# Fused attention and MLP on one core: key and query transposes by DMA from batch 3 on, and unread matmuls in the gaps of the head

## The chip, the cores and the metric

The kernel runs on one core of a Trainium2 chip. A core has five engines with a queue of instructions each, worked off strictly in order: TensorE (PE in the profile: matrix multiplications, and transposes as a multiplication with an identity matrix), VectorE (DVE), ScalarE (ACT), GpSimd (POOL) and SyncE (SP, which here only issues transfers). Sixteen DMA engines move data; transfers are issued from a queue of SyncE, ScalarE or GpSimd. SBUF is the on-chip memory of 128 partitions; PSUM is the small memory into which TensorE writes its results.

The metric is the device time of one execution in microseconds; less is better. Times of one kernel agree within some 0.3%.

## What is computed

Attention with a few extra "beacon" keys and values in front, then a two-layer MLP with an ELU between the layers. The reference, cut to what matters:

```python
B, H, S, Nb, D = 8, 8, 576, 16, 64
k_all = concatenate([beacon_k, k], axis=2)           # 592 keys per head
v_all = concatenate([beacon_v, v], axis=2)
scores = matmul(q, k_all.T) / sqrt(D)                # causal in the 576, beacons always seen
a = exp(scores - scores.max(-1)); a /= a.sum(-1) + 1e-9
x = matmul(a, v_all).transpose(0, 2, 1, 3).reshape(B * S, H * D)   # 4608 x 512
h = x @ w_in                                         # 512 x 2048
g = where(h > 0, h, exp(min(h, 0)) - 1)
out = g @ w_out                                      # 2048 x 512
```

All inputs and the output are float32 in memory. The kernel computes in bf16 and fp16.

## The kernel before

The unit of attention is a pair of heads of one batch, numbered n = 4 b + hp, 32 in all. The steps of a pair are:

1. `load_pair` (L263): one transfer each for k and q, 288 KB, issued by SyncE. 64 partitions hold nine consecutive tokens each, so that a packet is 2,304 bytes long. k goes to the even partitions of a staging tile (`st`, four of them), q to the odd ones. The beacon keys of a batch come by `load_bk` (L255).
2. `cast_pair` (L272): to bf16, on GpSimd for most pairs (L278), into one of two tiles `sb`. `cast_bk` does the beacon keys on GpSimd.
3. Transposes on TensorE: nine of 128x128 and one of the beacon keys per pair, `do_T` (L307, lines L311 and L313), into PSUM. Batch 0 uses `do_T2` (L317, L321 and L324), with the PSUM tiles of another tag.
4. Copies from PSUM to `kT` (L345, L346, VectorE) and `qT` (L351 on ScalarE or L353 on VectorE), which put the tokens back in order. There are four kT and four qT tiles (`NKQ`).
5. `do_SC` (L355): scores, keys by queries, 64 rows of the array per head, into PSUM (tag `sc`, two tiles).
6. `do_exp` (L368, ScalarE), `do_mask` (L375, GpSimd), then `do_AV` (L383): the numerator and, by a column of ones in v, the denominator. `do_norm` (L404, VectorE) divides and writes the rows of x. The values come by `load_v` (L285, 256-byte packets, 128 tokens by eight heads) and `cast_v`.
7. Transposes of x: for batches 0 and 1 on TensorE (`do_xT`, L422, with a copy in L433), from batch 2 on by a DMA transpose of 128 tokens by 512 columns (`turn_x`, L280, L282), five per batch.

The MLP goes by tiles of 512 tokens (two of 256 at the start). `do_mm1` (L444) makes 512 columns of h in PSUM (tile `hps`); `do_e` (exp, ScalarE), `do_clamp` (GpSimd) and `do_join` (VectorE) make the ELU (`gt`); `do_mm2` (L471) accumulates the output in PSUM (`ops`) in four quarters; `do_osb` copies it, and `do_store` stores it from SyncE's queue, through three tiles `osb`. A step of either multiplication is four 128x512 matmuls (eight of 256 columns in the first two tiles). The weights come by eight transfers with a cast, issued from GpSimd's queue (`load_w`, L298); `W_AFTER` says behind how many masks each stands there.

The order of the work is not that of the source. Each step is entered in a planner (`class Plan`) with an engine, a key (its wish for a place), a duration, what it depends on, and the buffers that it takes and gives. `Plan.run` goes through time as these durations have it: an engine that is free takes the ready step with the lowest key. The steps are then issued in the order found, and each engine's queue keeps it on the chip, whatever the true durations are. `SHIFT`, `AT`, `PACES` and the like are the constants behind the keys. Four PSUM banks of the tag `ff` serve in turn for `av`, `xt`, `tr2`, `hps` and `ops`.

Of the kernel before, what the change touches and what calls it, by code (L numbers as in the profile page):

```python
# [18 lines left out]
class Op:  # L19
    def __init__(self, eng, key, dur, fn, deps=(), take=(), give=(), mode=None, lat=0.03):  # L20
        self.eng, self.key, self.dur, self.fn = eng, key, dur, fn
        self.deps, self.take, self.give = [d for d in deps if d is not None], take, give
        self.mode, self.lat = mode, lat
        self.left, self.after = 0, []


class Plan:
# [10 lines left out]
    def run(self):  # L38
# [10 lines left out]
        mode = None  # L49
        for op in self.ops:  # L50
            if not op.left:
                heapq.heappush(ready[op.eng], (op.key, op.seq))
        events, order, now, n_left, tick = [], [], 0.0, len(self.ops), 0
        while n_left:
            for eng in ready:
                if free[eng] > now + 1e-9:
                    continue
# [19 lines left out]
                if op is None:  # L77
                    continue
# [15 lines left out]
            while events and events[0][0] <= now + 1e-9:  # L94
                _, _, op = heapq.heappop(events)
                if op is None:
                    continue
                n_left -= 1
                for t in op.give:
                    self.slots[t] += 1  # L100
                for o in op.after:
                    o.left -= 1
                    if not o.left:
                        heapq.heappush(ready[o.eng], (o.key, o.seq))
# [8 lines left out]
def kernel(  # L113
# [86 lines left out]
    NG, NET, NKQ = 20, 8, 4  # L200
# [22 lines left out]
    kTs = [big.tile([P, SKP], BF16, name=f"kT_{i}") for i in range(NKQ)]  # L223
    qTs = [big.tile([P, S], BF16, name=f"qT_{i}") for i in range(NKQ)]
# [5 lines left out]
    with tc.tile_pool(name="psum", bufs=1, space=bass.MemoryType.PSUM) as psum:  # L230
# [4 lines left out]
            "st": 4, "sb": 2, "bk": 1, "vst": 5,  # L235
        }
        plan = Plan(slots, {"PE": 16.0})
        add = plan.add
# [5 lines left out]
        def load(key, dur, fn, deps=(), take=(), issue=0.47):  # L244

            issue = add("SP", key, issue, fn, deps=deps, take=take)
            issues.append(issue)
            return add("DMA", key, dur, None, deps=[issue], lat=2.0)
# [6 lines left out]
        def load_bk(b):  # L255
            t = bks[b] = stage.tile([P, DM], FP32, tag="bk", name="bk32", bufs=1)
            nc.sync.dma_start(
                out=t[0:NB].rearrange("n (h d) -> n h d", h=H), in_=beacon_k[b].rearrange("h n d -> n h d"))
# [20 lines left out]

        def turn_x(b, blk):  # L280
            q0, rows, _ = BLOCKS[blk]
            nc.sync.dma_start_transpose(  # L282
                out=xTa[:, :, b * S + q0:b * S + q0 + rows], in_=x16s[b % 2][0:rows, blk, :])

        def load_v(b, jc):  # L285
            vst = vsts[b, jc] = stage.tile([P, H, D], FP32, tag="vst", name="vst", bufs=5)
            if jc == 0:
                nc.sync.dma_start(out=vst[0:NB], in_=beacon_v[b].rearrange("h n d -> n h d"))
            r0 = NB if jc == 0 else 0
            lo = P * jc - NB + r0  # L290
            n = kc_sz[jc] - r0
            nc.sync.dma_start(out=vst[r0:r0 + n], in_=v[b, :, lo:lo + n, :].rearrange("h s d -> s h d"))
# [191 lines left out]
        def do_store(tt, t4):  # L484
# [5 lines left out]
        SHIFT = [18.19, -1.67, -5.21, 9.28, 2.92, -5.56, -3.02, 18.21]  # L490
        AT = [-2.75, -0.54, -0.93, -0.06, 0.2, 1.01, 1.99, -16.61]
        AT0 = [[-45.78, -33.15, -38.79, -34.41], [-45.52, -23.75, -37.77, -41.96], [-33.6, -16.81, -31.44, -41.61]]
        PACES = [(-10.52, 1.48, 24.15, -2.31), (-10.42, 4.31, 27.52, 4.6), (37.71, 0.81, 11.65, 4.01), (83.94, 2.16, 31.7, 1.22), (112.53, 2.24, 29.18, 2.45)]
        W_AFTER = [[21.51, 12.09, 17.39, 6.76], [7.67, 24.47, 24.74, 25.24]]
        ON_POOL = "20010220"
        X_ON_ACT = "00"
        LAG = 17.55
        URGE = 72.32
        Q_ON_ACT = "01111110"
        FIRST = (  # L500
            "q2 k1 q1 v2 v1 k2 k3 q3 q5 v0 q4 k4 k5 v4 b1 v3 k6 q6 v6 v5 v9 q7 k7 v8 v7 ").split()

        def place(b, a):
            return 32 * (b - 1) + 8 * a + SHIFT[b]

# [11 lines left out]
        def plan_loads(n):  # L517
            b, hp = divmod(n, HP)
            if hp == 0:
                got = load(load_key(f"b{b}", place(b, 0) - 31), 0.2, partial(load_bk, b), take=["bk"])  # L520
                bk_in[b] = add("POOL", place(b, -0.9), 0.6, partial(cast_bk, b),
                               deps=[got] + last_T.get(b - 2, []), give=["bk"])
# [22 lines left out]
        def plan_w(which, f4):  # L545
            after = marks[max(0, min(len(marks) - 1, round(W_AFTER[which][f4])))]
            got = add("POOL", after.key + 0.01, 0.8, partial(load_w, which, f4), deps=[after])
            got = add("DMA", f4 - 300, 3.2, None, deps=[got], lat=2.5)
            w_at.update({(which, 4 * f4 + c): got for c in range(4)})

# [29 lines left out]
        def plan_pair(n):  # L580
# [3 lines left out]
            ready = plan_T2(n, key) if b == 0 else plan_T(n, key)  # L584
# [4 lines left out]
            for units, key in steps:  # L589
# [3 lines left out]
                last_kq[n] = SC  # L593
                first_SC.setdefault(n, SC)
# [13 lines left out]
            for r, groups in enumerate([(0,), (1,), (2,)] if b == 0 else [(0,), (1, 2)]):  # L608
# [11 lines left out]
                if b >= XB:  # L620
                    for blk in blks:
                        part.setdefault(blk, []).append(normed[-1])
                    if hp == HP - 1:
                        for blk in blks:
                            s = add("SP", at(AT[7]), 1.25, partial(turn_x, b, blk), deps=part.pop(blk))
                            done = add("DMA", at(AT[7]), 0.5, None, deps=[s], lat=2.2)
# [62 lines left out]
        for t in kTs:  # L689
            nc.vector.memset(t[:, SK:SKP], 0.0)  # L690
# [7 lines left out]
        for b in range(B):  # L698
            plan_v(b)
            for hp in range(HP):  # L700
                plan_loads(b * HP + hp)
                plan_pair(b * HP + hp)
# [39 lines left out]
```

## Time and profile before

| | us |
|---|---|
| median of 3 runs (368.13 to 369.10) | 368.67 |
| the profiled execution, device time | 367.97 |
| its span | 366.2 |
| busy: PE, DVE, ACT, POOL | 346.9, 213.3, 205.3, 190.6 |
| first MLP matmul (L449) starts | 35.57 |
| last matmul ends | 362.2 |

In the profile, times are microseconds from the start of the span unless marked ns; L449 is line 449 of the kernel before. A group line gives the line, the engine, the operation, what it writes and reads, the shape, and how many of them. The 40 slices give the busy share of an engine in tenths for each fortieth of the span, 9.155 us; PEclk is the granted TensorE clock in tenths of full speed. Matmuls are pipelined: a single one of 512 columns is shown as 0.38 us long though the next starts 0.22 us later, so the pitch between starts tells what one costs.

### The profile page before, as it was taken

The page shows a single profiled execution, that of the slowest core. Times are in us where ns is not written, and L with a number is a line of the kernel's source. Part 1 is how long each engine was busy: PE and PEld are TensorE (multiplying, and loading weights), DVE is VectorE, ACT ScalarE, POOL GpSimd, SP SyncE. Part 2 cuts the span into 40 slices and gives each one's busy share as a digit, 9 for nine tenths or more (in the row PEclk, how much of TensorE's full clock was granted, in tenths as well). Part 3 has the DMA queues.
Part 4 walks back from the last instruction along what each step waited for, and adds up shares of the span by engine and source line. Part 5 has one row for each costly group of instructions (what it writes and reads, how often), then busy time and mean ns, then how long its engine had stood idle before and what let it go on. Part 6 is the DMA issues. An engine that isn't in the chain of part 4 may idle for free.

```text
span 366.2 us, 8353 instructions
## 1 busy us (share of the span) xinstructions
PE 346.9 (95%) x3240; PEld 191.7 (52%) x3240; DVE 213.3 (58%) x454; ACT 205.3 (56%) x308; POOL 190.6 (52%) x363
## 2 busy tenths in 40 slices
PE   1796999999999999999999999999999999999995
PEld 1564775755465556555555554544555544444442
DVE  1575367778864777765756765555666554554321
ACT  3775683568857786767677666435546534333100
POOL 3383582658855866757466656335534434344200
PEclk9998799999999999999999999999999999999999
DMA  7999995788137966957696600220000221000022
GB/s 215 295 235 243 235 164 148 179 233 285 55 68 203 273 83 161 208 146 197 143 235 170 135 30 29 57 68 29 31 29 30 57 68 57 30 29 29 30 94 78
DMA packets 73256, 46.54 MB, mean 127 GB/s; under 512 B 56321, under 2 KB 60417, under 8 KB 73217
## 3 DMA queue, kind: packets, MB, share of 16 engines
q1 hardware_dynamic: 68848, 41.53, 43.4%
q0 software_dynamic: 4224, 4.19, 7.0%
q8 instruction: 25, 0.41, 0.5%
q10 hardware_dynamic: 144, 0.29, 0.2%
q14 instruction: 15, 0.11, 0.1%
HBM read 37.22 MB, written 9.44 MB: 127 GB/s over the span
## 4 chain that ended last, share of the span: by engine, by line
PE 86%; DMA 5%; DVE 2%; POOL 2%; ACT 2%; SPq 1%; issue 1%; ACTq 0%; DVEq 0%
PE ops L476 34%; PE hps L449 33%; PE sc L362 7%; PE av L396 7%; PE tr L311 3%; DMA w_in<-in_moe_w_in_dram 3%; DMA st<-in_q_dram 1%; POOL et L377 1%; PE tr L321 1%; DMA vst<-in_v_dram 1%; ACT et L371 1%; DVE kT L345 1%; DVE gt L468 1%; SPq L282 0%; DVE v L296 0%
## 5 line engine op out<-in xcount | busy, mean ns | idle before, releaser
L449 PE MATMUL hps<-xT,w_in 128*128 128x512 f16 (+1 forms) x640 | 146.0, 363 | 2.8 <-DMA w_in<-in_moe_w_in_dram 2.2
L476 PE MATMUL ops<-w_out,gt 128*128 128x512 f16 x576 | 144.2, 379 | 0.0
L468 DVE SCALAR_TENSOR_TENSOR gt<-e,hps 128x512 f16<-128x512 f32 x144 | 97.6, 684 | 79.5 <-POOL e L459 79.3
L459 POOL TENSOR_SCALAR e<-e 128x512 f32<-128x512 f32 x144 | 89.5, 624 | 104.3 <-ACT e L455 101.5
L455 ACT ACTIVATE e<-hps 128x512 f32<-128x512 f32 x144 | 85.5, 599 | 90.8 <-PE hps L449 86.9
L371 ACT ACTIVATE et<-sc 128x800 f16<-128x800 f32 (+3 forms) x128 | 103.9, 864 | 22.0 <-PE sc L362 18.8
L449 PEld LDWEIGHTS <-w_in 128*128 128x128 f16 x640 | 60.5, 99 | 59.3 <-DMA w_in<-in_moe_w_in_dram 2.3
L476 PEld LDWEIGHTS <-gt 128*128 128x128 f16 x576 | 52.4, 98 | 57.5 <-issue 3.0
L377 POOL TENSOR_SCALAR_AFFINE_SELECT et<-et 128x256 f16<-128x256 f16 (+2 forms) x160 | 60.0, 402 | 40.4 <-ACT et L371 37.3
L396 PEld LDWEIGHTS <-et 128*128 128x128 f16 (+1 forms) x960 | 37.3, 100 | 10.8 <-issue 1.9
L396 PE MATMUL av<-v,et 128*128 128x65 f16 (+1 forms) x960 | 41.5, 197 | 0.6 <-POOL et L377 0.6
L362 PE MATMUL sc<-qT,kT 64*128 64x80 bf16 (+3 forms) x704 | 37.2, 238 | 3.4 <-ACT et L371 1.8
L482 DVE COPY osb<-ops 128x512 f32<-128x512 f32 x36 | 24.8, 689 | 23.8 <-PE ops L476 23.6
L362 PEld LDWEIGHTS <-kT 64*128 64x128 bf16 x704 | 21.8, 97 | 25.4 <-issue 19.2
L412 DVE TENSOR_TENSOR x<-av,rl 128x256 f16<-128x256 f32 (+2 forms) x68 | 32.0, 471 | 2.3
L278 POOL CAST st<-st 128x1152 bf16<-128x1152 f32 x25 | 28.7, 1149 | 8.1 <-PE tr L313 6.4
L351 ACT ACTIVATE qT<-tr 128x576 bf16<-128x576 bf16 x24 | 15.6, 649 | 19.8 <-DVE kT L346 12.0
L345 DVE COPY kT<-tr 128x576 bf16<-128x576 bf16 x28 | 21.1, 754 | 8.1 <-PE tr L313 7.7
L411 DVE RECIPROCAL rl<-av 128x4 f32<-128x4 f32 (+2 forms) x68 | 12.5, 183 | 16.6 <-PE av L396 15.5
L296 DVE CAST v<-vst 128x512 f16<-128x512 f32 (+1 forms) x40 | 18.9, 489 | 4.3 <-DMA vst<-in_v_dram 4.3
L311 PEld LDWEIGHTS <-st 128*128 128x128 bf16 x252 | 16.1, 98 | 5.6 <-issue 0.4
L311 PE MATMUL tr<-identb,st 128*128 128x128 bf16 x252 | 18.6, 219 | 0.1
(32 smaller groups left out, 69.0 us busy)
## 6 DMA issues: line engine op xcount, KB each, us to landing
st<-in_k_dram SPq DMA_DIRECT2D x32, 288.0 KB, 4.2
out_dram<-osb SPq DMA_DIRECT2D x36, 256.0 KB, 2.1
st<-in_q_dram SPq DMA_DIRECT2D x31, 288.0 KB, 4.5
vst<-in_v_dram SPq DMA_DIRECT2D x24, 256.0 KB, 5.3
w_in<-in_moe_w_in_dram POOLq DMA_DIRECT2D x4, 512.0 KB, 9.0
w_out<-in_moe_w_out_dram POOLq DMA_DIRECT2D x4, 512.0 KB, 8.4
vst<-in_v_dram SPq DMA_DIRECT2D x8, 224.0 KB, 4.0
vst<-in_v_dram SPq DMA_DIRECT2D x8, 160.0 KB, 5.0
```

Of the source, the lines that this page charges most:

```text
L278: eng.tensor_copy(out=dst, in_=src)
L311: nc.tensor.transpose(out=tr[:, P * g:P * g + P], in_=b16s[n][:, g].rearrange("p h d -> p (h d)"), identity=identb)
L362: nc.tensor.matmul(out=sc[:, h, o:o + w], lhsT=kT[D * h:D * h + D, P * jc:P * jc + P], rhs=qT[D * h:D * h + D, q0:q0 + w], start=True, sto ...
L371: nc.scalar.activation(out=et[:, :, 0:w], in_=scs[n, u][:, :, 0:w], func=AFT.Exp, bias=0.0, scale=float(1.0 / (D ** 0.5)))
L377: nc.gpsimd.affine_select(out=et[:, :, c0:c0 + dw], in_=et[:, :, c0:c0 + dw], compare_op=ALU.is_ge, fill=fill0, base=q0 + NB - P * jc, pat ...
L396: nc.tensor.matmul(out=av[:, c:c + D + 1], lhsT=ets[n, CUT.unit_of[jc, at]][0:m, h, col:col + P], rhs=v16[0:m, jc, 2 * hp + h, 0:D + 1], s ...
L412: nc.vector.tensor_tensor(out=x16s[b % 2][:, blks[0]:blks[0] + nb, P * hp:P * hp + P].rearrange("q i (h d) -> q i h d", d=D), in0=av[:, :, ...
L449: nc.tensor.matmul(out=hps[:, (hi - lo) * j:(hi - lo) * (j + 1)], lhsT=w_in16[:, cc, P * fc:P * fc + P], rhs=xT[cc][:, lo:hi], start=(cc = ...
L455: nc.scalar.activation(out=e, in_=hpss[tt, i], func=AFT.Exp, bias=0.0, scale=1.0)
L459: nc.gpsimd.tensor_scalar(out=e, in0=e, scalar1=1.0, scalar2=0.0, op0=ALU.min, op1=ALU.max)
L468: nc.vector.scalar_tensor_tensor(out=gt, in0=es[tt, i], scalar=1.0, in1=hpss[tt, i], op0=ALU.subtract, op1=ALU.max)
L476: nc.tensor.matmul(out=ops, lhsT=gts[tt, fc][:, P * t4:P * (t4 + 1)], rhs=w_out16[:, fc, :], start=(fc == 0), stop=(fc == NFC - 1))
```

## The change

From batch 3 on (`PE_B`), keys and queries are no longer transposed on TensorE. They are loaded token by token like the values (128 tokens of all eight heads, beacon keys in front of the first chunk of keys), cast to bf16 two chunks at a time on VectorE or GpSimd (the string `TOK` says where), and turned by DMA transposes that write all four pairs at once. kT and qT become two tiles each, of four pairs. The planner has a second line of DMA work for the weights, served in turn with the first, a limit of nine transfers under way, and a filler: up to 34 us of its time, wherever TensorE has nothing ready and a `ff` bank is free, it issues a matmul of 256 columns on a tile of ones, the result of which is not read. The constants behind the keys are new, w_in's transfers stand earlier in GpSimd's queue, and some buffers are fewer.

```diff
@@ Plan.run
+                if eng == "DMA":
+                    if lines[0] or lines[1]:
+                        turn = 1 - turn if lines[1 - turn] else turn
+                        op = lines[turn].pop(0)
...
                 if op is None:
+                    if eng == "PE" and now < self.fill_until and self.slots["ff"]:
+                        mode = 0
+                        order.append((now, len(order), self.filler))
+                        free[eng] = now + self.filler.dur
...
-    NG, NET, NKQ = 20, 8, 4
+    NG, NET, NKQ = 18, 8, 2 * HP
+    PE_B = 3
...
-    kTs = [big.tile([P, SKP], BF16, name=f"kT_{i}") for i in range(NKQ)]
-    qTs = [big.tile([P, S], BF16, name=f"qT_{i}") for i in range(NKQ)]
+    kTa = [big.tile([P, HP, SKP], BF16, name=f"kT_{i}") for i in range(2)]
+    qTa = [big.tile([P, HP, S], BF16, name=f"qT_{i}") for i in range(2)]
+    kTs = [t[:, hp] for t in kTa for hp in range(HP)]
+    qTs = [t[:, hp] for t in qTa for hp in range(HP)]
+    ones = konst.tile([P, 2 * P], BF16, name="ones")
...
-            "st": 4, "sb": 2, "bk": 1, "vst": 5,
+            "st": 4, "sb": 2, "dq": 9, "vst": 4,
...
+        def do_fill():
+
+            spare = psum.tile([P, 512], FP32, tag="ff", name="spare", bufs=4)
+            nc.tensor.matmul(out=spare[:, 0:2 * P], lhsT=ones[:, 0:P], rhs=ones, start=True, stop=True)
+
+        plan.fill_until, plan.filler = 34.0, Op("PE", 0, 0.12, do_fill)
...
+        def load_tok(b, is_k, c):
...
+            if is_k and c == 0:
+                nc.sync.dma_start(out=t[0:NB], in_=beacon_k[b].rearrange("h n d -> n h d"))
+            nc.sync.dma_start(out=t[r0:r0 + n], in_=(k if is_k else q)[b, :, lo:lo + n, :].rearrange("h s d -> s h d"))
+
+        def cast_tok(b, is_k, c, m, eng):
+            o = b16s[b, is_k, c // 2] = stage.tile([P, G, 2, D], BF16, tag="sb", name="st16", bufs=2)
...
+            eng.tensor_copy(
+                out=o.rearrange("p g h d -> p (g h d)")[0:n, 0:DM * m],
+                in_=f32s[b, is_k, c // 2].rearrange("p h f -> p (h f)")[0:n, 0:DM * m])
+
+        def turn_tok(b, is_k, c):
+            r0, n, lo = rows_of(is_k, c)
+            t = (kTa if is_k else qTa)[b % 2]
+            nc.sync.dma_start_transpose(
+                out=t[:, :, P * c:P * c + r0 + n],
+                in_=b16s[b, is_k, c // 2].rearrange("p g h d -> p (g h d)")[0:r0 + n, DM * (c % 2):DM * (c % 2) + DM])
...
-        SHIFT = [18.19, -1.67, -5.21, 9.28, 2.92, -5.56, -3.02, 18.21]
+        SHIFT = [-1.59, -8.11, -4.8, -3.41, 4.52, 5.53, 8.01, 5.8]
...
-        W_AFTER = [[21.51, 12.09, 17.39, 6.76], [7.67, 24.47, 24.74, 25.24]]
+        W_AFTER = [[7.88, -52.99, -9.09, 6.95], [16.42, 25.9, 20.56, 31.58]]
+        DMA_AT = [-127.66, -67.18, 46.75]
+        TOK = ("111001", "010110", "101011", "011001", "000000")
...
+        def plan_tok(b):
+            turned[b] = []
+            for is_k in (True, False):
+                for c in range(0, NKC, 2):
+                    m = min(2, NKC - c)
...
+                    cast = add("DVE" if on_dve else "POOL", place(b, DMA_AT[0]) + i, 0.36 * m if on_dve else 0.53 * m,
+                               partial(cast_tok, b, is_k, c, m, nc.vector if on_dve else nc.gpsimd),
+                               deps=gots, take=["sb"], give=["st"])
+                    for j in range(m):
+                        s = add("SP", place(b, DMA_AT[1]) + i, 1.25, partial(turn_tok, b, is_k, c + j),
+                                deps=[cast] + last_SC.get(b - 2, []))
+                        turned[b].append(add("DMA", place(b, DMA_AT[1]) + i, 0.6, None, deps=[s],
+                                             give=["sb"] if j == m - 1 else [], lat=1.9))
...
-            ready = plan_T2(n, key) if b == 0 else plan_T(n, key)
+            ready = plan_T2(n, key) if b == 0 else plan_T(n, key) if b < PE_B else turned[b]
...
+        nc.vector.memset(ones, 1.0)
...
+            if b >= PE_B:
+                plan_tok(b)
             for hp in range(HP):
-                plan_loads(b * HP + hp)
+                if b < PE_B:
+                    plan_loads(b * HP + hp)
```

## The prediction

> **What bounds the kernel now.** I read the page's busy shares and 40 slices first, then the chain that ended last, then TensorE's timeline where the slices are not full, then stretches with few transfers in them, to price the DMA work.
>
> ```profile
> PE 346.9 (95%) x3240; PEld 191.7 (52%) x3240; DVE 213.3 (58%) x454; ACT 205.3 (56%) x308; POOL 190.6 (52%) x363
> PE   1796999999999999999999999999999999999995
> PEclk9998799999999999999999999999999999999999
> DMA  7999995788137966957696600220000221000022
> PE 86%; DMA 5%; DVE 2%; POOL 2%; ACT 2%; SPq 1%; issue 1%; ACTq 0%; DVEq 0%
> ```
>
> TensorE (PE) is full in all slices but the first four and the last; the chain lies on it for 86%. No other engine is above 58%. The DMA engines are full up to slice 7 (54 us), partly used to slice 23, then nearly idle. So from 48 us on TensorE's own work sets the end; before that it is the head.
>
> The timeline of TensorE (start, duration, count, and in brackets the idle time before it):
>
> ```profile
> 16.01 1.14 PE L321 MATMUL tr<-identb,st 128*128 128x128 bf16 x9 [0.55 <-POOL st L278]
> 35.57 5.30 PE L449 MATMUL hps<-xT,w_in 128*128 128x256 f16 x24 [2.15 <-DMA w_in<-in_moe_w_in_dram]
> 40.80 0.61 PE L362 MATMUL sc<-qT,kT 64*128 64x256 bf16 x14
> 48.63 2.79 PE L449 MATMUL hps<-xT,w_in 128*128 128x256 f16 x24
> 121.18 1.03 PE L449 MATMUL hps<-xT,w_in 128*128 128x512 f16 x4
> 122.04 0.67 PE L311 MATMUL tr<-identb,st 128*128 128x128 bf16 x9
> 122.54 0.22 PE L313 MATMUL tr<-identb,bk 128*128 128x128 bf16 x1
> 122.60 0.35 PE L396 MATMUL av<-v,et 128*128 128x65 f16 x6
> ```
>
> See the pitch, from start to start: the ten transposes of one pair of heads hold TensorE from 122.04 to 122.60. And see the same 24 matmuls take twice as long at 35.57 as at 48.63. The stretches (duration; busy PE, PEld, DVE, ACT, POOL; clock, DMA share, GB/s) show why, and what a transfer costs:
>
> ```profile
> 33.80:34.20 0.40, 0.00 (x0) 0.00 (x0) 0.00 (x0) 0.40 (x2) 0.24 (x1) 1.00 1.25 257
> 34.20:34.60 0.40, 0.00 (x0) 0.00 (x0) 0.00 (x0) 0.40 (x1) 0.40 (x2) 0.52 1.26 268
> 40.60:41.00 0.40, 0.40 (x6) 0.14 (x6) 0.40 (x1) 0.09 (x1) 0.00 (x0) 0.50 1.12 281
> 41.00:41.40 0.40, 0.40 (x15) 0.34 (x12) 0.22 (x1) 0.40 (x1) 0.00 (x0) 0.95 1.15 305
> 56.50:59.80 3.30, 3.30 (x36) 2.02 (x35) 1.94 (x6) 0.89 (x3) 0.00 (x0) 1.00 0.37 81
> 97.50:103.30 5.80, 5.80 (x77) 3.46 (x76) 4.17 (x9) 5.10 (x8) 4.47 (x10) 1.00 0.33 105
> 286.00:300.00 14.00, 14.00 (x93) 6.84 (x92) 7.46 (x14) 6.16 (x10) 5.96 (x11) 1.00 0.27 63
> ```
>
> The last matmul before the gap ends at 33.4; the granted clock halves at 34.2 and is back at 41.0, 5.5 us after TensorE became busy again.
>
> **The change, part by part.** The sum goes against the profiled execution: 367.97 us, of which 366.2 span and 1.77 around it. The median is 0.7 above that execution, so I add 0.7 at the end.
>
> *Transposes off TensorE.* Batches 3 to 7 have 20 pairs of ten transposes; by the timeline one set costs 0.56 us of a full engine: 20 x 0.56 = **-11.2 us**, all on the path. With them go 20 kT copies on VectorE (0.754 + 0.155 us each), 20 qT copies (about 0.65 on ScalarE, 0.75 on VectorE) and 20 casts (1.149 each on GpSimd). The new casts (30, of at most 1,024 columns) cost no more than those of 1,152 (0.750 on VectorE, 1.149 on GpSimd). These engines are below 60%, and the work is covered by TensorE; I count 0.
>
> *Their DMA work.* A load of 128 tokens has the shape of today's value load: the stretch at 56.5 holds one (with its beacon rows), 0.37 x 3.3 = 1.2 us. The stretch at 97.5 holds two of today's pair loads, 0.33 x 5.8 / 2 = 0.95 us each. The stretch at 286 holds five transposes and one store: 0.27 x 14 = 3.8 us; the store takes 0.7 (0.35 of a 2 us stretch at 302), so 0.62 a transpose. Per batch: 9 token loads 10.8 and 10 transposes 6.2, in place of 8 pair loads 7.6: +9.4 us, 47 over five batches. Between 60 and 220 us the DMA share averages 0.67, so some 53 us are free. It fits, with little left; where loads come too late the wait shows up on TensorE (below).
>
> *SyncE's queue.* 40 pair issues of 0.61 and five of bk go; 55 token and beacon issues of about 0.5 and 50 transposes of 1.25 us come: about +63 us, over some 170. Today this queue spends 119 us waiting for finished output tiles before a store, so it has the time. But it is strict in order, and now transposes of keys and queries stand behind those waits, and value loads and stores behind the transposes (a store one or two issues later is covered by the three osb tiles). Who waits in the end is the first score matmul of a batch: in the new order a batch's last transposes stand only a few issues ahead of its scores. Price: the x transposes land after 2.3 to 5.1 us, so a batch can lose 0 to 2.8, five batches 0 to 14. The only wait of TensorE shown from 48 to 345 us is one of 0.5 for a qT copy; taking 0.3 a batch, near that row, gives **+1.5**. A gain is excluded: nothing waits there now.
>
> *Unread matmuls in the head.* The built order holds 175 of them, all ahead of the first MLP matmul; 51 stand before the first transpose. They can't be skipped, so they set a floor to when that matmul comes. Their pitch is that of a 256-column matmul: 2.73/24 = 0.114 including gaps, 0.109 without, 0.213 at half clock. Start at about 1.2 (memset of the tile). If the clock is released after 5.5 us of dense work as at 41.0: 26 x 0.213 = 5.5, then 149 x 0.109 = 16.2. Real work ahead of it: 50 transposes 2.8, 86 score matmuls 3.2, 110 AV matmuls 3.4, 18 x transposes 0.9: 10.3. Some 16 changes between score and other matmuls at 0.11 (steps of 0.97 against 0.86 us in the chain): 1.8. Waits: 18 of the unread matmuls wait for a PSUM copy by another engine, since they pass through the same four banks as the real tiles, and the chain exp, mask, AV stays; I take 2.0, from 0 to 5. Sum 37.0, against 35.57: **+1.4** (34 to 41: -1.5 to +5.5). Twenty small matmuls move behind it: **+0.5**.
>
> *The clock.* If TensorE has no gap before it, the first MLP matmuls run at full clock: 24 in 2.73 in place of 5.23, and the 14 scores 0.1 less: **-2.6** (0 if a gap remains).
> In the Trainium skill, TensorE: Matmul & The Clock Gate, Part 1 lets the clock fall only after an idle window of about 3.4 us; by that rule a 2.15 us gap would have cost no clock and this term would be 0. The trace shows the clock halved 0.8 us after the last matmul, so the row decides.
>
> *Weights and loads in the head.* Two w_in loads now leave GpSimd's queue after the first pair's masks (about 11 us, against 19.8), ahead of the second pair's cast there; that cast is 0.8 later, covered by the unread matmuls, which hold that pair's transposes back to about 15. A weight load took up to 11.6 us to land, so w_in is there well before 37: the 2.15 wait is gone, already in the 37.0. Fewer gt and vst buffers: 0, no wait today names them; up to 1.
>
> Sum: 367.97 - 11.2 + 1.5 + 1.4 + 0.5 - 2.6 = 357.6, and 0.7: **358**.
>
> **The rivals.**
>
> *Transposes land late.* The cover of DMA and SyncE is thin: each of five batches then waits 1.2 to 2.8 instead of 0.3: 362 to 370, likeliest 364. For it: DMA slots near 0.9 while batches 3 to 7 load. Against: a batch's MLP work is 9/8 x 32 steps of 0.863 = 31 us, more than its 28 us of DMA (10.8 + 6.2 + value 5.5 + x 3.1 + stores 3.2).
>
> *The unread matmuls run at half clock.* Slower than before. If the clock isn't released in the head, all 175 cost 0.213 and the real work doubles: 37.3 + 20.6 + 1.2 + 3.8 = 63 for the first MLP matmul, 26 later than 37: 384. Each us at half clock beyond 6.7 loses half; the lead of 10 is gone if release comes after 27 us. For it: the transposes at 16.01 run at half pitch, and that stays so to about 26 us (the clock column says 1.00 until its first event; the pitch tells). Against: TensorE was only 76% busy there with gaps every us, and in the dense work at 35.57 it took 5.5 us.
>
> *DMA transposes are much slower than TensorE's.* If each 128x128 block were handled alone, for longer than 0.62/4 = 0.155 us, the loads would bind: a batch has 37 blocks, and at 0.7 us a block its DMA work (26 + 22) would exceed the 38 us of TensorE work (31 of MLP, 4 x 1.87 of scores and AV) by 10, 50 in all: above 400. Against: the 0.62 for four blocks.
> The Trainium skill, VectorE: DVE Perf Modes, The three transpose paths, gives 1,309 ns by DMA against 390 on TensorE for such a block, and advises TensorE if PSUM can take it; 37 of those would be an estimated 48 us a batch. The stretch at 286 disagrees.
>
> *No net effect.* The head loses 5.5, the clock stays halved after a gap, transposes wait 1 a batch: within 0.3%.
>
> **How the numbers follow.** Forecast 0.68 (own range 352 to 362); better than 351 (head below its low end, no new waits) 0.05; late transposes 0.16; no effect 0.03; half clock 0.05; slow blocks 0.03. Range **351 to 366**: outside lie 0.05 below, and above it the last three cases and 0.04 of the late transposes. 0.3% (1.1 us) is about what can be told from no change: faster 0.88 (the first two and 0.15 of the third), same 0.04, slower 0.08.
>
> **What would show it.** Groups: 20 fewer sets of ten transposes, 50 more DMA transposes from SyncE, 175 matmuls on the tile of ones. Timeline: unread matmuls at 0.213 for some 5 us from 1.2, then 0.109; the first MLP matmul at 34 to 41, 24 in about 2.7. Clock at 1.0 in all slices after the first. Waits of score matmuls for DMA under 1 us a batch. Wrong would make it: a clock of 0.5 in the head beyond 10 us, or idle TensorE ahead of the first scores of batches 3 to 7.

## The result, and the profile after

The changed kernel takes 382.62 us (median, 381.79 to 385.47), the kernel before 368.40 beside it: a ratio of 1.040 (95% interval 1.034 to 1.046). It is slower by 14 us, where 358 was predicted. Single runs of one version below spread by up to 8 us, more than the 0.3% said above. The profiled execution took 382.23 us, of which 380.5 are span.

The busy shares, three rows of slices (9.5 us each) and the chain that ended last, of the kernel after (line numbers from here on are those of the kernel after; in f2, g1b and the like they stand one or two lines lower):

```profile
PE 355.2 (93%) x3215; PEld 192.7 (51%) x3215; DVE 211.1 (55%) x433; ACT 192.4 (51%) x284; POOL 177.9 (47%) x352
PE   8999899999996996999949997789999999999995
PEclk9999999999999898999998999999999999999999
DMA  7999799875997669998775999782211210100012
PE 79%; DMA 8%; DVE 4%; SPq 3%; issue 2%; POOL 2%; ACT 1%; DVEq 0%; ACTq 0%; POOLq 0%
```

The head is filled as the change says. But TensorE's row has holes from 114 to 257 us where it had none, the clock dips there, and transfers, VectorE and SyncE's issues (SPq) take a larger part of the chain. TensorE's waits between 100 and 260 us (total, times, longest):

```profile
PE hps L514 <- DVE gt L533: 5.9, 3, 3.1
PE hps L514 <- DMA xT<-x: 4.9, 1, 4.9
PE hps L514 <- issue: 3.5, 1, 3.5
PE av L461 <- DVE gt L533: 2.4, 1, 2.4
PE av L461 <- DVE x L477: 0.8, 1, 0.8
PE ops L541 <- DVE osb L547: 0.5, 1, 0.5
```

These are 18 us, and not one is at a score matmul (sc), which is where the prediction expected them: the keys and queries come in time. The MLP matmuls wait, for x transposes and for what stands behind a cast on VectorE. TensorE's timeline shows what a wait costs beyond itself:

```profile
37.28 1.04 PE L514 MATMUL hps<-xT,w_in 128*128 128x256 f16 x8
...
123.37 3.57 PE L514 MATMUL hps<-xT,w_in 128*128 128x512 f16 x8 [3.51 <-issue]
...
146.20 2.54 PE L514 MATMUL hps<-xT,w_in 128*128 128x512 f16 x8 [3.05 <-DVE gt L533]
...
237.37 1.02 PE L514 MATMUL hps<-xT,w_in 128*128 128x512 f16 x4 [2.31 <-DVE gt L533]
```

Eight such matmuls take 1.83 us at full clock; at 123.37 they take 3.57. The stretches behind these three waits and the one of 4.9 us for xT, which ended at 198.45 (duration; busy PE, PEld, DVE, ACT, POOL; clock, DMA share, GB/s):

```profile
123.40:126.80 3.40, 3.40 (x8) 0.96 (x8) 0.20 (x1) 0.60 (x1) 1.41 (x4) 0.50 0.79 217
147.20:150.60 3.40, 3.40 (x13) 1.04 (x12) 1.71 (x3) 1.19 (x2) 1.65 (x2) 0.51 0.89 157
198.40:201.80 3.40, 3.35 (x8) 1.01 (x8) 0.11 (x1) 0.60 (x1) 1.47 (x4) 0.51 0.35 68
237.40:241.00 3.60, 3.60 (x49) 2.06 (x49) 2.45 (x7) 1.30 (x2) 1.00 (x1) 1.00 0.49 96
```

Three waits of 3.0 to 4.9 us each cost 3.4 us at half clock on top, 1.7 us of work; the wait of 2.3 us cost none. Now the chain of waits, in order of time, at the second hole:

```profile
139.03 1.10 DVE v L361 x2
140.26 1.26 SPq L347
141.57 3.53 DMA vst<-in_v_dram
146.20 2.54 PE hps L514 x8
```

A value load stands on SyncE's queue behind an x transpose (L347). It is issued at 141.57 and lands 3.5 us later. VectorE's timeline shows the cast that waits for it and the ELU join behind the cast, which TensorE waits for because it frees a PSUM bank:

```profile
145.13 0.43 DVE L361 CAST v<-vst 128x512 f16<-128x512 f32 x1 [3.75 <-DMA vst<-in_v_dram]
145.47 0.68 DVE L533 SCALAR_TENSOR_TENSOR gt<-e,hps 128x512 f16<-128x512 f32 x1
```

The longest wait, 4.9 us before 198.45, has a cast in its way too. In the chain, `DVE st L334` is a cast of the new token loads:

```profile
191.97 2.60 DMA kT<-st
194.68 0.69 DVE st L334
195.51 0.38 DVE x L477
195.90 2.50 DMA xT<-x
198.45 3.58 PE hps L514 x8
```

The cast writes one of the two tiles `sb`, and waits until a transpose of keys that reads it has landed. The norm of x (L477) stands behind the cast on VectorE, and the x transpose is issued only then.

SyncE's queue around the first hole (start, time that the row holds the queue, its waits inside that time included):

```profile
108.53 4.60 SPq L347 DMA_TRANSPOSE xT<-x  x2
113.17 0.58 SPq L328 DMA_DIRECT2D st<-in_q_dram  x1
113.86 2.51 SPq L341 DMA_TRANSPOSE kT<-st  x2
116.47 1.22 SPq L347 DMA_TRANSPOSE xT<-x  x1
117.77 2.97 SPq L341 DMA_TRANSPOSE qT<-st  x2
120.79 2.55 SPq L347 DMA_TRANSPOSE xT<-x  x2
```

The x transposes that TensorE needs at 120 stand behind transposes of keys and queries of the next batch. The profile names nothing that this wait waits for (`issue`). That it is these x transposes is read from the times: the median x transpose lands 2.5 us after its issue, and 120.79 + 2.5 is 123.3. Summed over such rows, SyncE's queue is held 18.8 to 19.3 us of each 20 from 100 to 200 us; before, it was 10 to 16. Held is not issuing all the time: the profile's list of this queue's waits from 100 to 240 us still has 39.5 us, against 72 before.

**The loss in the trace.** The version e2 below is the changed kernel with all keys and queries on TensorE; its span is 369.8, TensorE busy for 361.3. Against it the changed kernel has 16.8 us more idle time (25.3 against 8.5) and 6.1 less busy time. Of the latter, the transposes saved 11.2, and the three stretches at half clock cost 3 x 3.4 / 2 = 5.1. And 16.8 - 11.2 + 5.1 = 10.7, the difference of the spans. The saving is there; 22 us of waits and their clock came with it.

### The profile page after: what moved, and what is told of

The parts are those of the page before. It is cut to its first block, busy times and chain, and to the rows that moved or that the text cites. A ratio compares the mean times of both kernels' runs of the same rounds, so it can differ in the third digit from the quotient of the medians.

```text
span 380.5 us, 8245 instructions
## 1 busy us (share of the span) xinstructions
PE 355.2 (93%) x3215; PEld 192.7 (51%) x3215; DVE 211.1 (55%) x433; ACT 192.4 (51%) x284; POOL 177.9 (47%) x352
## 4 chain that ended last, share of the span: by engine, by line
PE 79%; DMA 8%; DVE 4%; SPq 3%; issue 2%; POOL 2%; ACT 1%; DVEq 0%; ACTq 0%; POOLq 0%
PE ops L541 30%; PE hps L514 28%; PE av L461 7%; PE sc L427 6%; PE spare L268 6%; DMA vst<-in_v_dram 5%; DVE gt L533 1%; DMA qT<-st 1%; POOL e L524 1%; SPq L341 1%; PE tr L376 1%; DVE v L361 1%; DMA kT<-st 1%; ACT et L436 1%; PE xt L487 1%
## 5 line engine op out<-in xcount | busy, mean ns | idle before, releaser
L436 ACT ACTIVATE et<-sc 128x736 f16<-128x736 f32 (+3 forms) x128 | 104.1, 864 | 39.0 <-PE sc L427 35.5
L461 PEld LDWEIGHTS <-et 128*128 128x128 f16 (+1 forms) x960 | 36.3, 97 | 15.6 <-issue 4.2
L461 PE MATMUL av<-v,et 128*128 128x65 f16 (+1 forms) x960 | 39.9, 193 | 3.5 <-DVE gt L533 2.4
L427 PE MATMUL sc<-qT,kT 64*128 64x80 bf16 (+3 forms) x704 | 35.4, 229 | 0.9 <-DVE qT L418 0.4
L477 DVE TENSOR_TENSOR x<-av,rl 128x384 f16<-128x384 f32 (+2 forms) x68 | 32.1, 472 | 2.3
L361 DVE CAST v<-vst 128x512 f16<-128x512 f32 (+1 forms) x40 | 20.7, 530 | 16.5 <-DMA vst<-in_v_dram 16.4
L268 PE MATMUL spare<-ones 128*128 128x256 bf16 x175 | 26.0, 282 | 1.6 <-DVE ones L778 1.3
L476 DVE RECIPROCAL rl<-av 128x6 f32<-128x6 f32 (+2 forms) x68 | 12.4, 182 | 14.3 <-PE av L461 13.9
L268 PEld LDWEIGHTS <-ones 128*128 128x128 bf16 x175 | 16.6, 101 | 6.4 <-issue 2.0
L334 POOL CAST st<-st 128x1024 bf16<-128x1024 f32 (+2 forms) x14 | 11.9, 852 | 16.4 <-DVE osb L547 6.2
L334 DVE CAST st<-st 128x1024 bf16<-128x1024 f32 (+2 forms) x16 | 11.2, 705 | 14.3 <-DMA kT<-st 7.5
L399 ACT ACTIVATE qT<-tr 128x256 bf16<-128x256 bf16 (+1 forms) x8 | 3.1, 453 | 9.1 <-PE tr L389 9.1
```

The costliest lines, as they stand in the source:

```text
L268: nc.tensor.matmul(out=spare[:, 0:2 * P], lhsT=ones[:, 0:P], rhs=ones, start=True, stop=True)
L427: nc.tensor.matmul(out=sc[:, h, o:o + w], lhsT=kT[D * h:D * h + D, P * jc:P * jc + P], rhs=qT[D * h:D * h + D, q0:q0 + w], start=True, sto ...
L436: nc.scalar.activation(out=et[:, :, 0:w], in_=scs[n, u][:, :, 0:w], func=AFT.Exp, bias=0.0, scale=float(1.0 / (D ** 0.5)))
L461: nc.tensor.matmul(out=av[:, c:c + D + 1], lhsT=ets[n, CUT.unit_of[jc, at]][0:m, h, col:col + P], rhs=v16[0:m, jc, 2 * hp + h, 0:D + 1], s ...
L477: nc.vector.tensor_tensor(out=x16s[b % 2][:, blks[0]:blks[0] + nb, P * hp:P * hp + P].rearrange("q i (h d) -> q i h d", d=D), in0=av[:, :, ...
```

## The experiments

The ratios are to the kernel before on the same chip, with 95% intervals. Not all versions ran on the same chip: a difference of two medians and the difference of their ratios disagree by up to 0.9 us.

| version | DMA batches | median us | ratio |
|---|---|---|---|
| changed kernel | 3 to 7 | 382.62 | 1.040 (1.034 to 1.046) |
| e1: no unread matmuls | 3 to 7 | 377.99 | 1.030 (1.026 to 1.034) |
| e2: all keys, queries on TensorE | none | 371.39 | 1.012 (1.008 to 1.016) |
| f4: e1 and e2 | none | 367.95 | 1.001 (0.999 to 1.003) |
| e4b: loads from ScalarE | 3 to 7 | 386.29 | 1.055 (1.048 to 1.062) |
| e5: planner told longer issues | 3 to 7 | 373.97 | 1.018 (1.013 to 1.024) |
| f1: x transposes on TensorE | 3 to 7 | 376.07 | 1.023 (1.019 to 1.026) |
| f2: half of each token load | 3 to 7 | 367.56 | 1.000 (0.996 to 1.003) |
| g1b: f4 and 50 unread transposes | none | 378.31 | 1.029 (1.024 to 1.035) |
| g2b: f4 and 45 unread loads | none | 371.57 | 1.013 (1.009 to 1.017) |
| f6: e1 and e5 | 3 to 7 | 375.37 | 1.022 (1.017 to 1.027) |
| f6: e1 and e5 | 4 to 7 | 364.26 | 0.991 (0.987 to 0.995) |
| **f6: e1 and e5** | **5 to 7** | **361.31** | **0.983 (0.978 to 0.987)** |
| f6: e1 and e5 | 6, 7 | 364.17 | 0.990 (0.987 to 0.993) |
| f5: e1 | 5 to 7 | 370.26 | 1.005 (1.002 to 1.009) |

The theory after the comparison was that SyncE's strict queue has no room for the new transposes; the rivals, that the DMA engines are full, that the order is bad, or that the loss lies with the unread matmuls.

### The two halves of the change, taken apart: e1, e2, f4

```diff
-        plan.fill_until, plan.filler = 34.0, Op("PE", 0, 0.12, do_fill)
+        plan.fill_until, plan.filler = 0.0, Op("PE", 0, 0.12, do_fill)
```

> The changed kernel without its 175 unread matmuls (the planner's filler is off). Theory S (SyncE's queue, full from 80 to 260 us, starves TensorE there): this changes the head alone. The first MLP matmul comes earlier than 37.3, but at half clock, so the head is worth the same within 3 us; the waits between 115 and 260 us stay. Time 379 to 386. Rival U (the unread matmuls are what costs, by holding the head back and shifting everything): the time falls by 8 us or more, to 375 or below.

```diff
-    PE_B = 3
+    PE_B = 8
```

> The changed kernel with keys and queries of all batches transposed on TensorE as before; unread matmuls, constants and buffers as in the change. Theory S: the 50 transposes and 20 more issues on SyncE are gone, its queue is below 70% busy between 80 and 260 us, and TensorE's waits there fall from 18 us to under 4. With 11.2 us of transposes back and the head of the change, 364 to 371. Rival C (the new constants and fewer buffers cause the waits): they stay, above 376.

f4 has both edits.

> All transposes of keys and queries on TensorE and no unread matmuls: what is left of the change is the constants, the buffers and the planner's second line. If the unread matmuls cost some 3.5 us as they did in the changed kernel: 371.4 - 3.5 = 367 to 369, no different from the kernel before. If the constants are worse by themselves: 370 or more.

e1 took 377.99, between its two expectations; e2 took 371.39, just above the range of theory S; f4 came as expected. The unread matmuls cost 3.8 us with five batches by DMA (1.0398 - 1.0296 of 368) and 4.2 with none (1.0123 - 1.0010). The rest of the change without them and without DMA transposes is no different from the kernel before. The first MLP matmul of e2 (first fence), and that of f4 with the longest wait behind it (second):

```profile
37.91 1.04 PE L514 MATMUL hps<-xT,w_in 128*128 128x256 f16 x8
```

```profile
33.27 1.04 PE L514 MATMUL hps<-xT,w_in 128*128 128x256 f16 x8
...
38.37 0.52 PE L427 MATMUL sc<-qT,kT 64*128 64x256 bf16 x14 [2.31 <-DVE qT L418]
```

Without unread matmuls the first MLP matmul comes 4.6 us earlier, and still at full clock (8 in 1.04): the gap ahead of it is gone without them. That w_in is sent earlier is the likely reason; no version tests it apart from the other new constants. The unread matmuls keep TensorE in order behind work that nobody needs. But f4, 2.3 us ahead of the kernel before at that matmul and at full clock, ends level with it: after 60 us neither waits longer than 0.6 us, so by then both had done the same work. TensorE in f4 is busy 2.7 us less in all (344.2), but idle 2.9 us more, most of it before 60 us. The start of the first MLP matmul doesn't measure the head.

### Another queue for the loads: e4b

```diff
-                nc.sync.dma_start(out=t[0:NB], in_=beacon_k[b].rearrange("h n d -> n h d"))
+                nc.scalar.dma_start(out=t[0:NB], in_=beacon_k[b].rearrange("h n d -> n h d"))
...
-            nc.sync.dma_start(out=vst[r0:r0 + n], in_=v[b, :, lo:lo + n, :].rearrange("h s d -> s h d"))
+            (nc.scalar if b >= PE_B else nc.sync).dma_start(out=vst[r0:r0 + n], in_=v[b, :, lo:lo + n, :].rearrange("h s d -> s h d"))
```

> The change, with the token loads and the value loads of batches 3 to 7 issued from ScalarE's queue in place of SyncE's: 85 issues of about 0.66 us, some 56 us, leave SyncE between 60 and 260 us; the DMA engines have the same work. Theory S: SyncE's share there falls from 0.96 to about 0.7, TensorE's waits after 100 us fall below 8 us, time 360 to 370. Rival D (the DMA engines are the bound: they are at 1.2 to 1.3 in some stretches): the waits stay, time above 378.

It took 386.29, in the range of the DMA theory, but its waits name another culprit:

```profile
PE sc L427 <- ACT et L436: 7.5, 7, 2.2
PE ops L541 <- DVE gt L533: 2.4, 1, 2.4
```

The exps stand behind load issues on ScalarE, which is in order too, and an issue there waits for its staging tile: ScalarE stood still for 7.7 us before one exp, until a transpose of keys had landed. SyncE's queue was held for only 111 of the 180 us from 60 to 240, and nothing was gained. The run doesn't tell SyncE from the DMA engines; it shows that an issue that waits holds up what stands behind it on ScalarE's queue too.

### Less on SyncE, less on the DMA engines: f1, f2

f1 turns x on TensorE in all batches:

```diff
-        XB = 2
+        XB = 8
...
-        X_ON_ACT = "00"
+        X_ON_ACT = "00000000"
```

> The changed kernel, but the x transposes of all batches on TensorE (as for batches 0 and 1). 30 DMA transposes of about 1.5 us each (45 us) leave SyncE's queue and no other engine's queue gets issues in their place; 18.6 us of DMA work go too. TensorE gets 120 more transposes, 120 x 0.056 = 6.7 us. Capacity theory (SyncE's queue, or the DMA engines, are full between 100 and 240 us): the waits of some 18 us and the half clock behind them (5 us) go: 382.6 + 6.7 - 18 to 23 = 366 to 371. Rival (the places of loads and casts in the order are bad, whatever the load on SyncE): waits stay, 378 or more.

f2 loads four heads of eight and casts them twice:

```diff
-            nc.sync.dma_start(out=t[r0:r0 + n], in_=(k if is_k else q)[b, :, lo:lo + n, :].rearrange("h s d -> s h d"))
+            nc.sync.dma_start(out=t[r0:r0 + n, 0:H // 2], in_=(k if is_k else q)[b, 0:H // 2, lo:lo + n, :].rearrange("h s d -> s h d"))
```

> The changed kernel, but a token load of batches 3 to 7 brings four of the eight heads, and the cast copies those four twice, so scores are computed from wrong keys and queries in half of the heads; all else is the same. The same number of issues, about half the packets: 45 x 0.6 = 27 us less DMA work between 60 and 230 us. If the DMA engines are what is short (share 1.05 to 1.3 in the stretches before the waits): the waits shrink, 365 to 374. If SyncE's queue is short and a token load's issue there stays near 0.7 to 1.0 us: 379 to 386. If the issue gets shorter with the number of packets, SyncE's busy time falls by up to 18 us of 160, and the two can't be told apart by the time alone.

f1 took 376.07, between the two expectations: the waits longer than 0.4 us, from 38 us on, fell from 18.8 to 9.0 us, at 6.7 us of work added to TensorE. f2 took 367.56, in the range of the DMA theory: half the packets are worth 15 us. Only one long wait is left (TensorE's timeline of f2):

```profile
142.90 3.44 PE L515 MATMUL hps<-xT,w_in 128*128 128x512 f16 x8 [3.52 <-DVE gt L534]
```

SyncE's queue shows why the two can't be separated here. Per row, a token load of queries held it for 0.99 us in the changed kernel and for 0.64 in f2 (medians 0.67 and 0.54), a transpose of keys for 1.54 and 1.40 (median 1.22 in both; the averages hold waits). Half the packets make less DMA work and a shorter hold. But the time that the queue is held, from 60 to 240 us, fell only from 167 to 162 us, and from 100 to 240 it is held 18.6 us or more of each 20 in f2 too. So a queue that is held nearly all the time is not the loss by itself. Whether f2 gains by earlier landings or by the few us on the queue is not shown.

### The disputed cost by itself: g1b, g2b

To f4, which has no transposes of keys and queries by DMA, unread traffic was added that nothing depends on. Five of the eight kT and qT buffers stay, to make room.

```diff
+        def turn_none(i):
+            nc.sync.dma_start_transpose(out=dts[i % 5], in_=ds)
+
+        for b in range(3, B):
+            for i in range(10):
+                s = add("SP", place(b, DMA_AT[1]) + i, 1.25, partial(turn_none, i), deps=[last_SC[b - 1][i * 8 // 10]])
+                add("DMA", place(b, DMA_AT[1]) + i, 0.6, None, deps=[s], lat=1.9)
```

> All keys and queries by TensorE, no unread matmuls (367.95), and 50 unread DMA transposes as before, but into five tiles in turn, so that none waits for the one before. They take 50 x 1.25 = 63 us of SyncE's queue (more if issues lengthen) and 31 us of DMA work, and no other step depends on them. If SyncE's issues by themselves are the price of the change: waits of x transposes and value loads, 374 to 382. If the queue has room for them as long as nobody's keys wait in it: 367 to 370.

```diff
+            nc.sync.dma_start(out=dls[i % 3], in_=k[b, :, P * (i % 4):P * (i % 4) + P, :].rearrange("h s d -> s h d"))
...
+            for i in range(9):
+                s = add("SP", place(b, 0) - 30 + i, 0.6, partial(load_none, b, i), deps=[last_SC[b - 1][i * 8 // 9]], take=["dq"])
```

> The same version with 45 unread token loads into three tiles in turn: 54 us of DMA work and 45 x 0.5 = 23 us of SyncE's queue. If the transfers are the price (the changed kernel has only some 16 us more DMA in its loads, since the pair loads go): 373 to 382. If there is room: 367 to 370.

g1b lies in the range for SyncE's issues as the price, g2b between its two ranges. The transposes cost 10.4 us against f4 (378.31 - 367.95), the loads 3.6 (4.3 by the ratios), though the loads bring more DMA work (54 us against 31, by the prediction's 1.2 and 0.62 each) and the DMA share from 100 to 140 us was 0.96 with them, 0.81 with the transposes. In the traces the 50 transposes held SyncE's queue for 76 us, the 45 loads for 35: 0.14 us lost per us of hold, and 0.10 to 0.12. Per us of DMA work it is 0.34 and 0.07 to 0.08. So the time on SyncE's queue is the better measure of the two, as far as two versions can show. g1b's TensorE shows the picture of the changed kernel, with no new dependence in it:

```profile
146.31 3.57 PE L516 MATMUL hps<-xT,w_in 128*128 128x512 f16 x8 [2.99 <-DVE gt L535]
```

A first attempt was flawed. All unread transfers went into one tile, so each waited in SyncE's queue for the one before:

```profile
SPq L801 <- DMA dt<-ds: 37.3, 19, 6.7
```

What was expected of the three:

> All keys and queries by TensorE and no unread matmuls (that version took 367.95), and added to it ten DMA transposes per batch 3 to 7 of 128 by 512 zeros into a tile that nobody reads, issued by SyncE, spread over the batch before. Nothing depends on them: they only take 50 x 1.4 to 1.5 = 70 to 75 us of SyncE's queue and 50 x 0.62 = 31 us of DMA work. SyncE's busy time between 60 and 240 us goes from 93 to about 165 of 180. Theory that the length of SyncE's queue is the price: waits of x transposes and value loads as in the changed kernel, 374 to 380. Theory that the DMA engines are the price: 31 us fit in between, 368 to 371. Theory that it was the dependences (the keys' own way through load, cast, transpose): 367 to 369.

> The same version, and added to it nine loads of 128 tokens per batch 3 to 7 (256-byte packets) into a tile that nobody reads: 45 x 1.2 = 54 us of DMA work and 45 x 0.66 = 30 us of SyncE's queue, to about 123 of 180 us. SyncE theory: the queue has room, 368 to 370. DMA theory: with the pair loads still there the DMA engines are as full as in the changed kernel or fuller, 372 to 380.

> Both additions: SyncE's queue would need some 195 of 180 us, and the DMA engines get 85 us more. If each price stands alone, the sum of the two losses; if a full DMA side also makes SyncE's issues longer, as the token loads' issues fell from 0.99 to 0.64 us with half the packets, more than the sum: 385 or more. If neither matters without the dependences: under 371.

They took 399.06 (transposes), 390.13 (loads; 383.68 to 391.84) and 441.16 (both). They price a wait inside the strict queue and not the issue: 37 us of such waits cost 21 us beyond the 378.31.

### The planner's lengths, and the number of batches: e5, f5, f6

```diff
-                        s = add("SP", place(b, DMA_AT[1]) + i, 1.25, partial(turn_tok, b, is_k, c + j),
+                        s = add("SP", place(b, DMA_AT[1]) + i, 1.6, partial(turn_tok, b, is_k, c + j),
...
-                            s = add("SP", at(AT[7]), 1.25, partial(turn_x, b, blk), deps=part.pop(blk))
+                            s = add("SP", at(AT[7]), 1.6, partial(turn_x, b, blk), deps=part.pop(blk))
```

Token and value loads likewise: 1.4 and 0.8 for 1.1 and 0.6, 1.3 and 0.65 for 1.0 and 0.5.

> The change, with the planner told that an issue on SyncE takes longer (a transpose 1.6 in place of 1.25 us, a token load 0.8 for 0.6, a value load 0.65 for 0.5); the same instructions in another order. Theory S, capacity: SyncE stays full, the waits move but stay, 374 to 384. Rival O (there is room enough, the order alone is wrong because the planner thinks SyncE faster than it is): the steps that wait stand later, waits under 8 us, time 358 to 370.

The new order alone is worth 8.6 us (7.9 by the ratios), with the work unchanged. The time lies at the lower end of the capacity theory and above the rival's range. The queue stays full, waits for values remain, and one wait of 1.4 us at a score matmul is for queries (TensorE's timeline of e5):

```profile
148.23 0.32 PE L461 MATMUL av<-v,et 128*128 128x65 f16 x3 [4.54 <-DVE v L361]
```

The f6 versions have these lengths and no unread matmuls, and take fewer batches by DMA:

```diff
-    PE_B = 3
+    PE_B = 5
...
-        TOK = ("111001", "010110", "101011", "011001", "000000")
+        TOK = ("101011", "011001", "000000")
```

> Keys and queries by DMA only in batches 6 and 7, no unread matmuls, and the planner told what SyncE's issues cost in the trace (1.6 us a transpose). Capacity theory: 20 transposes in place of 50, in the part of the run in which SyncE has most room and the DMA engines are nearly idle, so the 8 sets of ten transposes are a gain of 8 x 0.56 = 4.5 us against the version with none: 362 to 366. If DMA transposes are late in any case: 367 to 374.

> Keys and queries by DMA from batch 5 on (batches 6 and 7 only took 364.17), no unread matmuls, SyncE's issues told to the planner at their measured length. If SyncE's queue between 160 and 200 us (about 15 of 20 us busy with batches 6 and 7 alone) takes ten more transposes: 364.2 - 4 x 0.56 = 362. If it is full there: waits of 2 to 5 us come back, 364 to 370.

> DMA transposes from batch 4 on, no unread matmuls, measured issue lengths in the planner. With 0, 2 and 3 batches by DMA the times are 367.95, 364.17 and 361.31. If a fourth batch still fits beside the stores and x transposes: 361.3 - 2.2 = 359. If SyncE and the DMA engines are full from 120 us on: waits of 2 to 5 us come back, 361 to 367.

> The changed kernel with both cures, no unread matmuls and measured issue lengths in the planner; five batches by DMA. The two cures gave 4 us (378.0) and 8 us (374.0) one at a time: if they add, 382.6 - 4.6 - 8.6 = 369 to 371, no better than with no batch by DMA, since the waits for values and their casts (6.6 us with the planner's cure alone) stay. If waits go with four or fewer batches only, this one lies 6 us or more above the one with four.

> Three batches by DMA, no unread matmuls, and the planner's issue lengths as in the changed kernel. With five batches the measured lengths gave 8.6 us beside the unread matmuls and about 2.7 us without them. If the number of batches is what counts, SyncE's queue has room and the lengths matter little: 361 to 363. If the order that follows from the lengths is needed: 365 or more.

With 0, 2, 3, 4 and 5 batches: 367.95, 364.17, 361.31, 364.26, 375.37. From none to three the gain is 6.6 us for 12 sets of transposes, 0.55 a set: the 0.56 that the prediction took from the timeline (the version with none has the planner's old lengths). The fourth batch costs 3 us, the fifth 11. Five batches miss the 369 to 371 of adding the two cures. The same three batches with the old lengths take 370.26, 8 to 9 us more, and the waits are back (f5, TensorE's timeline):

```profile
188.42 1.90 PE L514 MATMUL hps<-xT,w_in 128*128 128x512 f16 x8 [1.29 <-DMA xT<-x]
...
227.65 1.02 PE L514 MATMUL hps<-xT,w_in 128*128 128x512 f16 x4 [2.18 <-DVE gt L533]
```

Between 60 and 260 us f5 has 8.0 us of idle TensorE, the three-batch f6 1.2; the rest of the difference is mostly a period at half clock behind the wait at 227.65 (1.7) and the head (1.5). That version, the best, in the busy shares and slices and, last, TensorE's only line of waits after 38 us:

```profile
PE 337.5 (94%) x3120; PEld 182.9 (51%) x3120; DVE 213.1 (59%) x444; ACT 195.8 (55%) x292; POOL 181.7 (51%) x355
PE   2688899999999999999999999899999999999995
PEclk9999999999999999999999999999999999999999
DMA  7999999998328486889479877992102310000022
PE hps L514 <- DVE gt L533: 1.7, 3, 0.9
```

It beats both kernels: 361.31 against 368.15 before, 1.7% less. Its queue on SyncE is also held for 18 to 19 us of each 20 from 140 to 240 us. So a full queue is no loss by itself; it is one when the order has what TensorE needs next behind what it needs a batch later. That lateness also grows with the length of the full stretch would explain the fourth and fifth batch (full from 120 and 100 us on); no version tests it alone.

## Why the prediction was wrong

- *Transposes off TensorE, -11.2*: right. The busy times add up with it, and 0.55 a set was measured over three batches.
- *SyncE's queue, +1.5*: the step that failed. It set +63 us against "119 us waiting" as if that time could be used anywhere. Only 18 of the 119 us lie between 100 and 240 us, where all waits of SyncE's queue were 72 us, and such a wait helps only if it stands ahead of the instruction that would otherwise be late. It named the wrong place too: "Who waits in the end is the first score matmul of a batch". The x transposes and value loads were late. The step had put the value loads behind the transposes and then covered the stores alone; x transposes behind those of keys and queries it did not name. In place of 1.5 the runs show 22 us, 16.8 of waits and 5.1 of half clock behind them. Issues and transfers that nothing depends on cost 10 (g1b), an order planned with issues that are too short 8 to 9 (e5, f5). These are not two parts of a sum: g1b was planned with the short lengths as well, and with the unread matmuls away the lengths give 2.6 us at five batches and 8 to 9 at three. How the 22 us divide stays open.
- *The new casts, 0*: "the work is covered by TensorE" looked at how busy VectorE is and not at its order. A cast that waits for a tile `sb` holds up the norm of x behind it; through it goes the longest wait, 4.9 us and 1.7 of clock.
- *Their DMA work, 0*: "It fits, with little left" took the mean share of 0.67 over 160 us. In the changed kernel the share is 0.86, 1.00 and 0.77 in the three stretches of 40 us from 100 on, and halving the token loads gave 15 us. Against the DMA engines as the only cause stands g2b, where a share of 0.96 and 0.87 from 100 to 180 cost 4 us. How much of f2's gain is the engines' own lateness, and how much SyncE's shorter holds, stays open.
- *Unread matmuls, +1.4 and +0.5*: the floor was right (37.0 predicted, 37.28), in part by luck: the first 51 unread matmuls took 6.86 us, by the prediction's two pitches some 13 at half clock and not 26, 1.4 us less, and the rest took 1.6 longer. The sum was not right. With the clock's -2.6 the head was to gain 0.7; e2 is 4.5 us slower than the kernel before. The missed term is that the unread matmuls stand in the way of real work that would be ready earlier: without them, with w_in's earlier place in GpSimd's queue, the matmul came at 33.3 to 33.9.
- *The clock, -2.6*: seen as said in the head (8 matmuls in 1.04), but f4 shows that it takes no unread matmul in front of it (e1 lost some clock earlier in the head, below), and another 5.1 us went to half clock behind later waits, which the prediction had priced without it.
- *The rivals*: "Transposes land late" had the right kind, thin cover, with a price of 1.2 to 2.8 a batch. It was 22 / 5 = 4.4, and it was x and the values that came late, not the keys; the clock is added. "Half clock" in the head and "much slower" transposes fell: the clock was full from about 4 us on (by the 51 matmuls above), and the saving came out at its price where the queue had room. The 1,309 ns a block by DMA of the Trainium skill, VectorE: DVE Perf Modes, The three transpose paths, are not borne out as a cost per block in a stream: three batches by DMA ran without a wait of TensorE for a key or a query.

## What to carry over

Before moving work to a queue, look at that queue in the stage where the work goes and name every instruction that will stand behind it; idle time elsewhere in a strict queue is no room. Move as much as the stage can carry and no more, with the planner told the measured lengths: so planned and without unread matmuls, three batches gained 6.8 us on the kernel before, where five lost 8. And judge a filled head by when the real work is done, not by when a milestone starts.

## What the runs showed of the hardware

Half clock came in periods of 3.4 us, one or several on end. In the changed kernel waits of 2.3 and 2.4 us left the clock alone, and those of 3.05, 3.5 and 4.9 us each cost one such period, which began 3.5 to 4.9 us after the last matmul; at the second hole that was 1.0 us after TensorE was busy again. The Trainium skill, TensorE: Matmul & The Clock Gate, Part 1, says that the clock is set by a free-running window of 3,413 ns. These traces agree in the length. They don't agree that a whole idle window is needed (the same part): a wait of 2.41 us cost a period in the f6 version with five batches, two of 1.20 and 1.87 us close together did in e4b, and the gap of 2.15 us in the head of the kernel before halved the clock for 6.8 us, two periods, from 0.8 us after the last matmul. In the head of e1 the clock was halved from 21.5 to 28.2 us, though TensorE had no gap longer than 0.8 us in the nine before; f4, with nearly the same head, came to full clock at about 24 us (14 matmuls of L461 in 0.58 us at 24.46, against 0.98 at 24.27 in e1) and kept it. So the length of one gap does not decide: a wait below 2.6 us may or may not cost 1.7 us of work or more, and all of 2.7 us and more did here. The prediction took the 0.8 us of one gap for the rule, which it isn't.

A load of 128 tokens held SyncE's queue for 0.99 us on average with all its packets and for 0.64 with half of them (medians 0.67 and 0.54). Whether that follows the packets of the load itself or how full the DMA engines are is not separated. A DMA transpose held it for 1.2 us at least.
